# Issuing the sine half of the rotated q and k transfers from ScalarE's queue

## The chip, the cores and the metric

The kernel runs on one core of a Trainium2 chip. A core has five engines that run side by side, each with its own queue of instructions worked in order: TensorE (PE, matmuls; its weight loads are listed as PEld), VectorE (DVE), ScalarE (ACT), GpSimd (POOL) and SyncE (SP, which here only issues transfers). An engine waits at the head of its queue until what the instruction needs is there. Transfers are done by 16 DMA engines; some engine has to issue each. The metric is the device time of one execution in microseconds (us), lower is better.

## What is computed

The reference has two parts. The first is a gated linear attention with complex decay, per batch (4) and head (8), over 768 positions with 48 channels:

```python
mag = np.sqrt(a_re * a_re + a_im * a_im)
scale = np.minimum(mag, 0.999) / (mag + 1e-06)
a_re_n, a_im_n = (a_re * scale, a_im * scale)
for t in range(S):
    new_re = ar * S_re - ai * S_im
    new_im = ar * S_im + ai * S_re
    kv = np.einsum('bhd,bhe->bhde', k[:, :, t], v[:, :, t])
    S_re, S_im = (new_re + kv, new_im)
    y[:, :, t] = np.einsum('bhd,bhde->bhe', q[:, :, t], S_re)
```

(`ar`, `ai` are the scaled decay of position t.) The second takes the 3072 rows of 384 that come out of it through a feed-forward layer with weights of 384 x 2048 and 2048 x 384:

```python
h = x @ w_in
g = h * (1.0 / (1.0 + np.exp(-1.702 * h)))
return (g @ w_out).astype(np.float32)
```

## The kernel before

**Units.** The 4 x 768 positions are cut into 12 units of 256, numbered u = 0 to 11; three units make a batch entry. A unit goes through three stages. `prepare` turns the decay into factors: running products and running angles of each channel, the cosine and sine of the angles, and q and k scaled by the products and multiplied with cosine and with sine. `attend` computes scores, masks them and forms the outputs and the running state in two halves of 128 positions. `moe` does the feed-forward layer in eight slices i of 256 hidden columns, each in two halves f. This text writes Hu.i.f for the hidden product of a half (L794, nine matmuls; three of float32 in unit 0), g for its activation on ACT (L807, L803 in unit 0), and Ou.i.f for the output product (L827, six matmuls). There are two PSUM buffers for H, taken in turn by the slices, so H of slice i waits until g of slice i - 2 has been read.

**The transfers in question.** `prepare` works with channels on partitions, `attend` with heads beside each other. In between, transfers inside SBUF bring the products to rows per head, in `remap` (L658 to L667): five DMAs from one source tile, which holds 256 columns of q, 256 of k and one of decay (1539 elements a row for three row groups). There are two source tiles: x = 0 is `qr`, the products with the cosine, and goes to rows 0 to 47 of `qkh`; x = 1 is `qk`, the products with the sine, and goes to rows 64 to 111. Both hold q and k columns, so the two halves differ in cosine and sine. Unit 0 is prepared in two parts of 128 positions, so there are 13 cosine and 13 sine blocks of five DMAs. The scores (p_ps, L702) and the turned keys (k_ps, L748, copied by ACT to `kt`, L759) read `qkh`.

**Weights.** The float64 words of the weights come in 16 tiles (A0 to A7 of w_in, U0 to U7 of w_out), in the order A0, A1, U0, A2, U1, A3, U2, A4, U3, A5, U4, A6, U5, A7, U6, U7, through four buffers `raw`. Each is loaded (L472), one step on ACT (L474) and three on DVE (L475, L478, L481) make float32 of it, and only then can its buffer be loaded again. Later steps split the tiles in a high and a low half (L494, L499). All this happens while unit 0 is under way.

**The order.** All steps are first collected by `add` with an engine, a guessed duration, a rank and the tiles they read and write. `Plan.order` then runs a list scheduler over them many times and keeps the order that its own cost function likes best; the instructions are written out in this order, so each engine's queue is fixed at build time. The scheduler treats SP by itself (L176 to L180): a step there is a DMA, or `work` of them, and frees SP at once but for the issues.

Of the kernel before, what the change touches and what calls it, by code (L numbers as in the profile page):

```python
# [21 lines left out]
P = 128  # L22
L = 128
HL = 64
T = 256
H = 8
D = 48
NR = 3
# [5 lines left out]
E0 = 32  # L34
# [42 lines left out]

def lag(a, b):
    return LAG if b != "PE" else 0.0 if a == b else LAG_PE


class Plan:
# [31 lines left out]
    def forward(self, rank, stay):  # L114
# [16 lines left out]
        while done < len(ops):  # L131
# [41 lines left out]
                continue  # L173
            can[e].remove(pick)
            heapq.heapify(can[e])
            if e == "SP":  # L176
                free[e] = s + 0.06 + 0.65 * (ops[n][8] - 1)
                hw = max(hw, s + 0.06) + 0.47 * ops[n][8]
                dma = max(dma, hw + 0.6) + dur
                end = dma + 0.9  # L180
            else:
                if ops[n][5] not in (None, table):
                    dur += max(0.0, LOAD - (s - idle))
                    table = ops[n][5]
                if e == "PE":
                    dur += CHANGE if kinds[n] != kind else 0.0
                    kind = kinds[n]
                free[e] = end = clock.end(s, dur, ops[n][8]) if e == "PE" else s + dur
            if e == "ACT":
                idle = end  # L190
                if ops[n][7] is not None:
                    todo[ops[n][7]] -= 1
                    held = ops[n][7] if todo[ops[n][7]] else None
# [9 lines left out]
    def backward(self, when):  # L203
# [14 lines left out]
        while done < len(ops):  # L218
# [35 lines left out]
            else:  # L254
                n = heapq.heappop(can[e])[1]
            dur = ops[n][1]
            if e == "SP":
                free[e] = s + max(dur, 0.47)
                end = s + 0.9 + dur + 1.13
            else:  # L260
                if ops[n][5] not in (None, table):
                    dur += LOAD if table else 0.0
                    table = ops[n][5]
                free[e] = end = s + dur
# [9 lines left out]
    def time(self, order, load):  # L274

        ops = self.ops
        free = dict(FREE)
        ends = [0.0] * len(ops)
        table, hw, dma, idle = None, 0.0, 0.0, 0.7
        clock = Clock()  # L280
        kinds, kind = self.kinds, None
        for n in order:
            e, dur = ops[n][0], ops[n][1]
            s = max([free[e]] + [ends[d] + lag(ops[d][0], e) for d in ops[n][4]])
            if e == "SP":
                free[e] = s + 0.06 + 0.65 * (ops[n][8] - 1)
                hw = max(hw, s + 0.06) + 0.47 * ops[n][8]
                dma = max(dma, hw + 0.6) + dur
                ends[n] = dma + 0.9
                continue  # L290
            if ops[n][5] not in (None, table):
                dur += max(0.0, load - (s - idle))
                table = ops[n][5]
            if e == "PE":
                dur += CHANGE if kinds[n] != kind else 0.0
                kind = kinds[n]
            free[e] = ends[n] = clock.end(s, dur, ops[n][8]) if e == "PE" else s + dur
            if e == "ACT":
                idle = s + dur
        return max(ends)  # L300
# [37 lines left out]
def attention_moe(ctx: ExitStack, tc: tile.TileContext, qk_in, v, a_in, w_in, w_out, qn, kn, vn, an, bn, out):  # L338
# [185 lines left out]
    def prepare_part(u, i, a, b, np_, mag, den, rec, sp, qm, th, *keys):  # L524
# [4 lines left out]
        def ks(*xs):  # L529
            return [f"{x}.{s}" for x in xs for s in sub]  # L530
# [3 lines left out]
        def rk(stage):  # L534
            return prep_rank(u, i, stage)
# [107 lines left out]
        for x, (dst, kd, fac, kf) in enumerate(((rv, "qr", cs, k_cs), (qv, "qk", t, k_th))):  # L643
            for j in range(2):
                both(f"rot{x}{j}", u, i, rk(f"rot{x}"), qj[1 - x][j], qj[0][j], fac, ALU.mult,
                     r=ks(f"qk{j}") + kf, w=ks(f"{kd}{j}"))
            if u == i == 0 and x == 1:
                for k in range(WARM):
                    add("PE", 0.43, -WARM + k, lambda k=k, dst=dst: mm(
                        h_ps[0][:, k % 2, :], lhsT=ident, rhs=dst[:, k % NR, 0:T], start=True, stop=True  # L650
                    ), r=["qk0.0", "qk1.0"], w=["h0.0", "h0.1"])
            if b == T:
                add("POOL", 0.13, rk(f"rot{x}"), lambda dst=dst: pool.tensor_copy(out=dst[:, :, 2 * n], in_=f_a[:, u, :]),
                    r=[f"fa{u}.{i}"], w=[f"{kd}1.1"])
            add("SP", REMAP * nn / (2 * T), rk(f"rot{x}"), lambda dst=dst, x=x: remap(u, x, o, nn, dst),
                r=ks(f"{kd}0", f"{kd}1"), w=[f"H{hb_(u)}.{s}.{x}" for s in sub], name=f"remap{u}.{i}.{x}", work=5)

    def remap(u, x, o, nn, src):  # L658


        dst = qkh[hb_(u)][64 * x : 64 * x + D, H * o : H * (o + nn)].rearrange("d (h x) -> d h x", h=H)
        rest = D - E0
        for j in range(2):
            dma(out=dst[:, j * NR : (j + 1) * NR, :], in_=src[j * D : (j + 1) * D, :, :])  # L664
        dma(out=dst[0:E0, 2 * NR : H, :], in_=src[2 * D : P, 0:NR:2, :])
        for j in range(2):
            dma(out=dst[E0:D, 2 * NR + j, :], in_=src[2 * D + j * rest : 2 * D + (j + 1) * rest, 1, :])  # L667

    def attend(u):
        sps = spans(u)  # L670
# [497 lines left out]
```

## Time and profile before

| what | us |
|---|---|
| median of 3 runs | 593.93 |
| lowest and highest | 593.01, 596.69 |
| the profiled execution | 601.2 |
| its span, first to last instruction | 599.4 |
| PE busy in the span | 556.5 |
| DVE busy | 484.9 |
| ACT busy | 279.6 |
| mean granted clock of PE | 0.994 |

A profile is one execution, with the profiler on. Rows of the timeline begin with the start in us from the span's begin and the length in us, then engine, line, operation, output tile <- input tiles and a count; what stands in brackets is how long the engine had been idle and which work ended the wait. `SPq` is SP's queue, issuing a DMA; the transfer itself goes on after that. Lines are those of the kernel before. The DMA engines move 78.46 MB in the span, 77.52 MB of it from one queue, SP's.

### The profile page before, as it was taken

The page shows a single profiled execution, that of the slowest core. Times are in us where ns is not written, and L with a number is a line of the kernel's source. Part 1 is how long each engine was busy: PE and PEld are TensorE (multiplying, and loading weights), DVE is VectorE, ACT ScalarE, POOL GpSimd, SP SyncE. Part 2 cuts the span into 40 slices and gives each one's busy share as a digit, 9 for nine tenths or more (in the row PEclk, how much of TensorE's full clock was granted, in tenths as well). Part 3 has the DMA queues.
Part 4 walks back from the last instruction along what each step waited for, and adds up shares of the span by engine and source line. Part 5 has one row for each costly group of instructions (what it writes and reads, how often), then busy time and mean ns, then how long its engine had stood idle before and what let it go on. Part 6 is the DMA issues. An engine that isn't in the chain of part 4 may idle for free.

```text
span 599.4 us, 14244 instructions
## 1 busy us (share of the span) xinstructions
PE 556.5 (93%) x5804; PEld 513.8 (86%) x5804; DVE 484.9 (81%) x1003; ACT 279.6 (47%) x468; POOL 26.3 (4%) x75
## 2 busy tenths in 40 slices
PE   0489959999999999999999999999999999999997
PEld 0367637999998999989999989988999989999997
DVE  7999859998968988979979789869979889555543
ACT  7877457546337354354373552552473542211210
POOL 4110001000101000000010000000001000000000
PEclk9999979999999999999999999999999999999999
DMA  8479972272283362374670861772670732732110
GB/s 336 140 253 345 213 180 78 57 153 68 71 187 97 86 160 96 92 157 135 126 208 19 177 198 37 150 223 57 138 201 19 153 129 68 137 86 70 63 45 30
DMA packets 31525, 78.46 MB, mean 131 GB/s; under 512 B 4448, under 2 KB 9568, under 8 KB 31456
## 3 DMA queue, kind: packets, MB, share of 16 engines
q1 hardware_dynamic: 31456, 77.52, 48.3%
q8 instruction: 46, 0.75, 0.5%
q14 instruction: 23, 0.19, 0.1%
HBM read 53.87 MB, written 4.72 MB: 98 GB/s over the span
## 4 chain that ended last, share of the span: by engine, by line
PE 76%; DMA 10%; DVE 8%; ACT 2%; SPq 2%; issue 1%; DVEq 0%; ACTq 0%
PE h_ps L794 30%; PE o_ps L827 30%; PE x_ps L728 6%; PE p_ps L702 5%; DMA raw_w<-in_w_out_dram 4%; DMA raw_w<-in_w_in_dram 3%; PE k_ps L748 2%; PE z_ps L755 2%; DMA raw<-in_w_in_dram 2%; SPq L667 1%; DVE fit L854 1%; DVE s L616 1%; DMA raw<-in_w_out_dram 1%; SPq L664 1%; DVE qk L456 1%
## 5 line engine op out<-in xcount | busy, mean ns | idle before, releaser
L807 ACT ACTIVATE g<-h_ps 128x256 f32<-128x256 f32 x176 | 62.6, 382 | 219.6 <-PE h_ps L794 132.5
L794 PE MATMUL h_ps<-xhi,hiA 128*128 128x256 f32 x528 | 151.6, 287 | 1.6 <-issue 1.1
L794 PE MATMUL h_ps<-xlo,hiA 128*128 128x256 f32 x528 | 149.0, 282 | 0.0
L794 PE MATMUL h_ps<-xhi,loA 128*128 128x256 f32 x528 | 149.0, 282 | 0.0
L794 PEld LDWEIGHTS h_ps<-xhi,hiA 128*128 128x128 f32 x528 | 100.2, 190 | 4.0 <-issue 2.1
L794 PEld LDWEIGHTS h_ps<-xhi,loA 128*128 128x128 f32 x528 | 100.5, 190 | 0.0
L794 PEld LDWEIGHTS h_ps<-xlo,hiA 128*128 128x128 f32 x528 | 100.4, 190 | 0.2
L827 PE MATMUL o_ps<-hiU,gh 128*128 128x384 f32 x352 | 93.9, 346 | 1.4 <-DVE osb L838 1.0
L827 PE MATMUL o_ps<-loU,gh 128*128 128x384 f32 x352 | 89.6, 335 | 0.0
L827 PE MATMUL o_ps<-hiU,gl 128*128 128x384 f32 x352 | 89.6, 335 | 0.0
L810 DVE CAST gh<-g 128x256 fp32r<-128x256 f32 x176 | 48.9, 288 | 39.9 <-ACT g L807 35.6
L812 DVE TENSOR_TENSOR gl<-g,gh 128x256 fp32r<-128x256 f32 x176 | 72.1, 422 | 5.6
L827 PEld LDWEIGHTS o_ps<-loU,gh 128*128 128x128 f32 x352 | 63.7, 188 | 0.0
L827 PEld LDWEIGHTS o_ps<-hiU,gl 128*128 128x128 f32 x352 | 63.6, 188 | 0.0
L827 PEld LDWEIGHTS o_ps<-hiU,gh 128*128 128x128 f32 x352 | 58.2, 189 | 5.6 <-issue 2.0
L854 DVE TENSOR_REDUCE fit<-raw_w 128x1 f32<-128x256 f32 x96 | 38.2, 413 | 25.5 <-DMA raw_w<-in_w_out_dram 16.3
L456 DVE TENSOR_TENSOR qk<-qk,s 128x768 f32<-128x768 f32 (+1 forms) x52 | 46.0, 892 | 0.2
L1005 ACT ACT_TABLE_LOAD x35 | 44.9, 1283 | 1.4 <-PEq L1156 0.8
L702 PEld LDWEIGHTS p_ps<-qkh 128*64 128x64 f32 x768 | 36.4, 136 | 10.4 <-issue 4.5
L702 PE MATMUL p_ps<-qkh 128*64 128x128 f32 (+1 forms) x768 | 42.7, 252 | 2.2 <-DVE pm L706 2.2
L706 DVE TENSOR_TENSOR pm<-p_ps,mask 128x512 f32<-128x512 f32 x48 | 33.0, 688 | 10.8 <-PE p_ps L702 10.5
L728 PE MATMUL x_ps<-pm,v 128*32 128x128 f32 x768 | 38.2, 278 | 1.5 <-DVE pm L706 1.4
(94 smaller groups left out, 753.3 us busy)
## 6 DMA issues: line engine op xcount, KB each, us to landing
v<-in_v_dram SPq DMA_DIRECT2D x24, 352.0 KB, 4.0
ri<-in_a_dram SPq DMA_DIRECT2D x11, 768.0 KB, 5.0
qk<-in_qk_dram SPq DMA_DIRECT2D x11, 768.0 KB, 5.1
qkh<-qr SPq DMA_DIRECT2D x22, 288.6 KB, 5.8
qkh<-qk SPq DMA_DIRECT2D x22, 288.6 KB, 7.3
raw<-in_w_in_dram SPq DMA_DIRECT2D x8, 768.0 KB, 7.5
raw<-in_w_out_dram SPq DMA_DIRECT2D x8, 768.0 KB, 8.4
raw_w<-in_w_in_dram SPq DMA_DIRECT2D x24, 256.0 KB, 2.8
```

Of the source, the lines that this page charges most:

```text
L456: add(en, t, rank, lambda: e.tensor_tensor(out=out, in0=a, in1=b, op=alu), **kw)
L702: mm(p_ps[to : to + HL, j, lo:L], lhsT=at(h, 1, c)[:, lo : lo + HL], rhs=at(h, 0, c)[:, lo:L], start=True, stop=True)
L706: add("DVE", d_t(CW), rk(4 * c + hh), lambda hh=hh: dve.tensor_tensor(out=pm[hh].rearrange("p (a b) t -> p a b t", b=2), in0=p_ps.rearrang ...
L728: mm(x_ps[32 * j : 32 * j + 32, r, :], lhsT=lt, rhs=rt, start=n == 0, stop=n == len(steps) - 1)
L748: nc.tensor.transpose(k_ps[:, j, 0:KD], at(4 * hh + j, 1, c)[0:KD], ident[0:KD, 0:KD])
L794: mm(h_ps[hb][:, f, :], lhsT=ww[:, r * T + f * P : r * T + (f + 1) * P], rhs=x[:, r, :], start=n == 0, stop=n == last)
L807: add("ACT", a_t(T) - 0.15, rk(i), lambda hb=hb, f=f: act(out=g32[:, f, :], in_=h_ps[hb][:, f, :], func=AF.Silu, scale=SLOPE), r=[f"h{hb}. ...
L810: add("DVE", d_t(T, 2), rk(i), lambda gb=gb, f=f: dve.tensor_copy(out=high.g(gb)[:, f, :], in_=g32[:, f, :]), r=[f"g.{f}"], w=[f"gh{gb}.{f}"])
L812: add("DVE", d_t(T), rk(i), lambda gb=gb, f=f: dve.tensor_tensor(out=glo[gb][:, f, :], in0=g32[:, f, :], in1=high.g(gb)[:, f, :].bitcast(F ...
L827: mm(o_ps[t], lhsT=x[:, f, t * L : (t + 1) * L], rhs=y[:, f * DM : (f + 1) * DM], start=i == 0 and f == 0 and n == 0, stop=i == NP - 1 and ...
L854: add("DVE", d_t(CK), rk + 2, lambda x=x, op=op: dve.tensor_reduce(out=f_w[:, x, n : n + 1], in_=weights.looked_at()[:, :, 1], op=op, axis ...
L1005: nc.scalar.preload_act_table_set(o[5])
```

## The change

The sine blocks (x = 1) are issued from ACT's queue, the cosine blocks stay with SP. `remap` picks the queue by x, and the step is added to ACT with a kind "dma". The planner's three passes take such a step on ACT as an issue: it holds ACT for 0.65 us a DMA in the planner's count, and ends when the transfer has landed.

```diff
+def issue(e, n):
+    return 0.06 + 0.65 * (n - 1) if e == "SP" else (0.65 if e == "ACT" else 1.0) * n
...
-            if e == "SP":
-                free[e] = s + 0.06 + 0.65 * (ops[n][8] - 1)
+            if e == "SP" or kinds[n] == "dma":
+                free[e] = s + issue(e, ops[n][8])
                 hw = max(hw, s + 0.06) + 0.47 * ops[n][8]
                 dma = max(dma, hw + 0.6) + dur
                 end = dma + 0.9
+                if e == "ACT":
+                    idle = free[e]
...
-            add("SP", REMAP * nn / (2 * T), rk(f"rot{x}"), lambda dst=dst, x=x: remap(u, x, o, nn, dst),
-                r=ks(f"{kd}0", f"{kd}1"), w=[f"H{hb_(u)}.{s}.{x}" for s in sub], name=f"remap{u}.{i}.{x}", work=5)
+            add("ACT" if x else "SP", REMAP * nn / (2 * T), rk(f"rot{x}"), lambda dst=dst, x=x: remap(u, x, o, nn, dst),
+                r=ks(f"{kd}0", f"{kd}1"), w=[f"H{hb_(u)}.{s}.{x}" for s in sub], name=f"remap{u}.{i}.{x}", work=5, kind="dma")
...
+        queue = (nc.sync, nc.scalar)[x].dma_start
         for j in range(2):
-            dma(out=dst[:, j * NR : (j + 1) * NR, :], in_=src[j * D : (j + 1) * D, :, :])
-        dma(out=dst[0:E0, 2 * NR : H, :], in_=src[2 * D : P, 0:NR:2, :])
+            queue(out=dst[:, j * NR : (j + 1) * NR, :], in_=src[j * D : (j + 1) * D, :, :])
+        queue(out=dst[0:E0, 2 * NR : H, :], in_=src[2 * D : P, 0:NR:2, :])
```

Since the planner counts otherwise, the order changes on every engine, not only at the moved steps. Lines of the new kernel are 8 to 9 higher here (L664 becomes L673, L472 becomes L480). Three places matter below.

On SP at the start, before: the cosine and sine blocks of both parts of unit 0 stand in one row, and the next weight loads behind them.

```order
L664 DMA qkh_75<-qr 48x768 x2
L665 DMA qkh_75<-qr 32x2x256
L667 DMA qkh_75<-qr 16x256 x2
L664 DMA qkh_75<-qk 48x768 x2
L665 DMA qkh_75<-qk 32x2x256
L667 DMA qkh_75<-qk 16x256 x2
L664 DMA qkh_75<-qr 48x771 x2
L665 DMA qkh_75<-qr 32x2x257
L667 DMA qkh_75<-qr 16x257 x2
L664 DMA qkh_75<-qk 48x771 x2
L665 DMA qkh_75<-qk 32x2x257
L667 DMA qkh_75<-qk 16x257 x2
```

On ACT at the same place, now: both sine blocks stand behind the last sine of unit 0 (L650) and ahead of a square for unit 1, a weight step and the two `kt` copies.

```order
L650 ACTIVATE s_85<-s_85 128x3x128
L673 DMA qkh_75<-qk 48x768 x2
L674 DMA qkh_75<-qk 32x2x256
L676 DMA qkh_75<-qk 16x256 x2
L673 DMA qkh_75<-qk 48x771 x2
L674 DMA qkh_75<-qk 32x2x257
L676 DMA qkh_75<-qk 16x257 x2
L440 ACTIVATE s_81<-ri 128x3x256
L482 ACTIVATE raw_73<-raw_73 128x768
L768 ACTIVATE kt_97<-k_ps 128x448
L482 ACTIVATE raw_74<-raw_74 128x768
L768 ACTIVATE kt_97<-k_ps 128x448
```

Ten issues have gone from SP's row into ACT's, ahead of steps that PE's attention of unit 0 waits for.

On SP around unit 1's blocks, before: the load of A7 (into `raw_72`) stands between the cosine and the sine block, those of U6 and U7 behind both.

```order
L472 DMA raw_71<-in_w_out_dram 128x1536
L664 DMA qkh_75<-qr 48x1539 x2
L665 DMA qkh_75<-qr 32x2x513
L667 DMA qkh_75<-qr 16x513 x2
L472 DMA raw_72<-in_w_in_dram 128x1536
L664 DMA qkh_75<-qk 48x1539 x2
L665 DMA qkh_75<-qk 32x2x513
L667 DMA qkh_75<-qk 16x513 x2
L472 DMA raw_73<-in_w_out_dram 128x1536
L472 DMA raw_74<-in_w_out_dram 128x1536
```

The same place on SP now:

```order
L480 DMA raw_71<-in_w_out_dram 128x1536
L480 DMA raw_72<-in_w_in_dram 128x1536
L673 DMA qkh_75<-qr 48x1539 x2
L674 DMA qkh_75<-qr 32x2x513
L676 DMA qkh_75<-qr 16x513 x2
L480 DMA raw_73<-in_w_out_dram 128x1536
L480 DMA raw_74<-in_w_out_dram 128x1536
```

A7's load has moved ahead of the cosine block; U6's and U7's now follow it directly, and the sine block is no longer in this row.

On ACT in the feed-forward layer of unit 1, now: the sine block of unit 2 stands between the two g of slice 4 (h_ps_106 is the buffer of even slices), where before the g followed each other.

```order
L816 ACTIVATE g_98<-h_ps_107 128x256 x2
L816 ACTIVATE g_98<-h_ps_106 128x256
L673 DMA qkh_76<-qk 48x1539 x2
L674 DMA qkh_76<-qk 32x2x513
L676 DMA qkh_76<-qk 16x513 x2
L816 ACTIVATE g_98<-h_ps_106 128x256
L816 ACTIVATE g_98<-h_ps_107 128x256 x2
```

The other nine later blocks stand likewise between two g.

More of the change, by code (lines that the diff above doesn't have):

```diff
@@ L189, in forward @@
             if e == "ACT":
-                idle = end
+                idle = free[e]
                 if ops[n][7] is not None:
@@ L256, in backward @@
             dur = ops[n][1]
-            if e == "SP":
-                free[e] = s + max(dur, 0.47)
+            if e == "SP" or self.kinds[n] == "dma":
+                free[e] = s + max(dur if e == "SP" else 0.0, issue(e, ops[n][8]), 0.47)
                 end = s + 0.9 + dur + 1.13
@@ L284, in time @@
             s = max([free[e]] + [ends[d] + lag(ops[d][0], e) for d in ops[n][4]])
-            if e == "SP":
-                free[e] = s + 0.06 + 0.65 * (ops[n][8] - 1)
+            if e == "SP" or kinds[n] == "dma":
+                free[e] = s + issue(e, ops[n][8])
                 hw = max(hw, s + 0.06) + 0.47 * ops[n][8]
@@ L289, in time @@
                 ends[n] = dma + 0.9
+                if e == "ACT":
+                    idle = free[e]
                 continue
@@ L662, in remap @@
         rest = D - E0
+        queue = (nc.sync, nc.scalar)[x].dma_start
         for j in range(2):
-            dma(out=dst[:, j * NR : (j + 1) * NR, :], in_=src[j * D : (j + 1) * D, :, :])
-        dma(out=dst[0:E0, 2 * NR : H, :], in_=src[2 * D : P, 0:NR:2, :])
+            queue(out=dst[:, j * NR : (j + 1) * NR, :], in_=src[j * D : (j + 1) * D, :, :])
+        queue(out=dst[0:E0, 2 * NR : H, :], in_=src[2 * D : P, 0:NR:2, :])
         for j in range(2):
-            dma(out=dst[E0:D, 2 * NR + j, :], in_=src[2 * D + j * rest : 2 * D + (j + 1) * rest, 1, :])
+            queue(out=dst[E0:D, 2 * NR + j, :], in_=src[2 * D + j * rest : 2 * D + (j + 1) * rest, 1, :])
     def attend(u):
```

## The prediction

> **What bounds the kernel now.** I read the slices of the page first, then who waited for whom on TensorE (PE), then the chain of waits and the timeline where PE waits. In the slices (40 of 15 us) PE is full from the seventh on:
>
> ```profile
> PE   0489959999999999999999999999999999999997
> DVE  7999859998968988979979789869979889555543
> ACT  7877457546337354354373552552473542211210
> DMA  8479972272283362374670861772670732732110
> ```
>
> ```profile
> PE h_ps L649 <- DVE qk L456: 23.3, 1, 23.3
> PE h_ps L794 <- ACT g L803: 7.1, 1, 7.1
> PE p_ps L702 <- DVE pm L706: 2.2, 2, 1.3
> ```
>
> The waits of PE (us in total, times, longest) are two: 23.3 us before its first instruction and 7.1 us once. All that the change can win lies before some 100 us. The windows say the same (length, then busy us of PE, PEld, DVE, ACT, POOL; PE clock; DMA share; GB/s):
>
> ```profile
> 74.80:79.80 5.00, 0.00 (x0) 0.00 (x0) 0.00 (x0) 0.00 (x0) 0.00 (x0) 0.81 1.03 149
> 82.00:110.00 28.00, 28.00 (x333) 21.11 (x334) 25.69 (x41) 20.79 (x30) 2.22 (x5) 0.95 0.26 89
> 110.00:500.00 390.00, 384.71 (x4176) 364.14 (x4176) 335.23 (x699) 184.11 (x304) 12.86 (x45) 1.00 0.49 123
> ```
>
> From 74.8 to 79.8 no engine works and the DMA engines are full at 149 GB/s. The timeline shows why:
>
> ```profile
> 62.17 1.18 SPq L664 DMA_DIRECT2D qkh<-qr  x2
> 66.71 0.52 SPq L472 DMA_DIRECT2D raw<-in_w_in_dram  x1
> 67.94 3.10 SPq L664 DMA_DIRECT2D qkh<-qk  x2
> 70.75 1.45 PE L827 MATMUL o_ps<-valU,g 128*128 128x384 f32 x4
> 72.04 1.46 PE L794 MATMUL h_ps<-x,valA 128*128 128x256 f32 x6
> 73.23 1.51 SPq L667 DMA_DIRECT2D qkh<-qk  x2
> 79.81 0.56 DVE L475 TENSOR_SCALAR valA<-raw 128x768 int32<-128x768 int32 x1 [6.32 <-DMA raw<-in_w_in_dram]
> 79.87 0.92 ACT L474 ACTIVATE raw<-raw 128x768 int32<-128x768 uint32 x1 [7.59 <-DMA raw<-in_w_in_dram]
> 81.84 2.93 PE L794 MATMUL h_ps<-x,valA 128*128 128x256 f32 x6 [7.05 <-ACT g L803]
> 84.69 0.89 PE L702 MATMUL p_ps<-qkh 128*64 128x128 f32 x16
> ```
>
> ```profile
> 66.71 13.08 DMA raw<-in_w_in_dram
> ```
>
> The load of weight tile A7 is issued at 66.71 behind unit 1's cosine transfers and takes 13.08 us among them and the sine transfers; ACT stands in L474 for it, so the g that frees PE's buffer is late. PE waits 7.05 us, and the six matmuls behind the wait take 2.93 instead of 1.46: together 8.5 us.
>
> **The change, part by part.** It removes and adds no computation: 65 DMA issues go from SP to ACT, and the planner writes another order on every engine.
>
> Start of the work on PE:
>
> ```profile
> 21.71 1.23 SPq L664 DMA_DIRECT2D qkh<-qr  x2
> 23.31 7.51 PE L649 MATMUL h_ps<-qk,ident 128*128 128x256 f32 x26 [23.31 <-DVE qk L456]
> 25.05 1.17 SPq L664 DMA_DIRECT2D qkh<-qk  x2
> 30.66 0.55 PE L748 MATMUL k_ps<-ident,qkh 112*128 112x112 f32 x4
> 31.24 0.55 ACT L759 ACTIVATE kt<-k_ps 128x448 f32<-128x448 f32 x1
> 43.06 0.47 ACT L736 ACTIVATE x<-x_ps 128x384 f32<-128x384 f32 x1
> 49.53 1.21 ACT L803 ACTIVATE g<-h_ps 128x256 f32<-128x256 f32 x4
> 49.97 2.85 PE L827 MATMUL o_ps<-valU,g 128*128 128x384 f32 x8 [0.43 <-ACT g L803]
> ```
>
> A half's five issues take SP 25.05 - 21.71 = 3.3 us. The sine half waits for SP until 25.05; on ACT it goes out at about 23.2, when DVE has rotated it, and is 1.9 us earlier. That wins nothing: the 26 warm-up matmuls wait for the same rotation and hold PE until 30.7. I take 0, between 0 and +0.5. ACT pays for it: ten issues, 6.6 us, stand in front of a square, a weight step and the kt copy of 31.24.
>
> What ACT and DVE take for the steps that change places (a DVE step of the chain of waits each, one ACT step of the timeline, the table loads of the page):
>
> ```profile
> 53.27 0.47 DVE valA L475
> 53.74 0.87 DVE valU L481
> ```
>
> ```profile
> 80.69 0.83 ACT L494 ACTIVATE hiA<-valA 128x768 fp32r<-128x768 f32 x1
> ```
>
> ```profile
> L1005 ACT ACT_TABLE_LOAD x35 | 44.9, 1283 | 1.4 <-PEq L1156 0.8
> ```
>
> In the new order ACT has, between unit 0's second x copy and its first g, five steps like L494 (0.83), three L474 (0.92), the kt copy (0.55) and two table loads (1.28): 10.0 us, where the old one took 49.53 - 43.53 = 6.0. The copy itself comes earlier: of DVE's steps one like L475 and about 5.5 like L481, 5.4 us in all, move behind the last mask product ahead of it. I count half, 2.7. The term is 10.0 - 6.0 - 2.7 = **+1.3**, between -1.4 (all 5.4) and +5.4 (ten issues that end 4.1 later, see the second rival).
>
> The stall. A7's load now stands ahead of unit 1's cosine transfers, and the sine transfers have their own queue. Then its 13.08 us go to some 7, and the 7.05 of waiting and the 1.47 of slow matmuls go: **-8.5**, between -8.5 and 0. What is late next? ACT issues the five sine transfers between g of slices 4 and 5 of unit 0, 3.9 us (below). PE has about as much of its own there, an output half and two hidden halves, but the g ahead comes late too, behind ACT's step for A7: **+1.0**, between 0 and +3.8 (the five issues from 67.94 on took 6.8, to 74.74, 2.9 more). PE would then ask for unit 1's rotated rows at about 81.4: 74.79, plus 1.46 for the second half of slice 6, plus 2.85 for the output product that the new order puts first, plus 1.3 and 1.0.
>
> But those rows leave later than before. ACT comes to the issue behind g of slice 4, which PE's output half of 70.75 takes, now 70.75 + 1.3 + 1.0 = 73.0, and behind A7's L474 of 0.92: at 73.9 (before: 67.94). It ends at 77.8. How long the last piece flies:
>
> ```profile
> qkh<-qk SPq DMA_DIRECT2D x2, 32.1 KB, 9.4
> qkh<-qk SPq DMA_DIRECT2D x2, 32.1 KB, 5.5
> ```
>
> The first row is the DMA view of 60 to 80 us, the second that of 105 to 150 (copies, KB, median us to landing). So they land between 83.3 and 87.2, and PE, with half a us of z before it, waits 1.4 to 5.3. I take **+3.4**, the middle, since two weight loads stand beside them and not three. Last, U6's load now stands behind the cosine transfers where A7's stood; DVE may wait for it up to 6.3 us as it did for A7, most of it beside PE's own wait: **+1.0**, between 0 and +6.3.
>
> Units 1 to 10. Each has one such block on ACT. How long it is, and what PE has to do meanwhile:
>
> ```profile
> 160.53 1.16 SPq L664 DMA_DIRECT2D qkh<-qr  x2
> 164.44 1.16 SPq L664 DMA_DIRECT2D qkh<-qk  x2
> 203.68 1.16 SPq L664 DMA_DIRECT2D qkh<-qr  x2
> ```
>
> ```profile
> 113.33 2.17 PE h_ps L794 x18
> 115.50 4.16 PE o_ps L827 x24
> ```
>
> Rows 1 and 2 (timeline) give 3.9 us for five issues, the last two (chain of waits) 1.08 us for one hidden half and 1.04 for one output half. At the tightest place, unit 1, PE has after H1.4.1 (unit, slice, half) three hidden and four output halves, 7.4 us, before it needs that half's buffer again; ACT, blocked 3.9 us from 0.7 us before H1.4.1's end, has g ready at 3.6. So **0**. Nothing in the order stands between the sine rotation on DVE and this place, so ACT should not wait for data. The new order's own gaps I bound by what PE lacks in the window of 110 to 500 us, 390 - 384.71 = 5.3 us, either way.
>
> Sum: 1.3 - 8.5 + 1.0 + 3.4 + 1.0 + 0 = -1.8. The span goes from 599.4 to 597.6 and the profiled execution from 601.2 to 599.4; the median of the runs shown, 593.93, is 7.3 below that execution and becomes **592.1**.
>
> **Rivals.** *The stall goes whole.* If the sine rows, on a queue of their own, have landed when PE comes, the last two terms fall: -6.2, and -8.5 without the two delays on ACT: 587.7 to 585.4. For it: the landings of 5.5 us where the DMA engines have room. Against: the DMA row of the slices has 9 from 45 to 75 us.
>
> *Two queues share one issuer.* Then SP's and ACT's issues take turns. The twenty at the start end at 21.7 + 20 x 0.62 = 34.1 and not at 23.2 + 10 x 0.66 + 0.2 of waiting = 30.0, all behind them on ACT comes 4.1 later, the first term is +5.4 and the sum +2.3: 596.2. For it: rows of SP issue back to back at 0.6 us each, and nothing in this trace issues from two queues at once. Against: no row shows whether that 0.6 belongs to SP or to something shared. The Trainium skill, "Perfetto Trace Analysis", section "DMA Instruction — HWDGE (DVE, Sync)", says that such an instruction first waits for a lock on a generator of descriptors that the queues share; by that rule this rival holds. "DMA: Bandwidth & Descriptors", section "Issuing engines are not separate DMA queues", adds that transfers of all issuers run on the same 16 engines and that only issuing time is saved, which speaks against the first rival. No run so far shows either.
>
> *DVE becomes the bound.* While ACT issues, DVE stands at its next cast of g. A unit takes 43.2 us (160.53 to 203.68); DVE works 335.23 of 390, or 37.1 of 43.2, so ACT's block fits up to 6.1 us a unit. At 6.8 (67.94 to 74.74) each of ten units would lose 0.7, at twice 3.9 1.7: +7 to +17 on the sum of -1.8, so 599 to 609, middle 604. For it: DVE's order puts other steps behind a cast that waits. Against: outside the full stretch SP shows 3.9.
>
> **How the numbers follow.** Forecast 0.44 (own range 589 to 595), the stall goes whole 0.21, shared issuer 0.22, DVE bound 0.13. A measurement of this kernel tells about 1%, 5.9 us, from no change. Faster by more: the first rival, 0.21. Slower by more: the last, 0.13. The rest, 0.66. The range reaches from the first rival's end over the shared issuer's 596.2 with its gaps of 3.7: 585.4 to 600.
>
> **What would show it.** In the changed profile: PE's first k_ps near 30.7; first g of unit 0 at 50 to 51; no wait of 7 us before L803; instead a wait of PE at unit 1's p_ps for rows still in flight, its p_ps between 83 and 88; five issues on ACT of about 3.9 us in later units and no new wait of PE there. I am wrong if PE is full before 80, if an issue on ACT takes much over 0.8 us, or if PE's gaps after 110 us grow past 10 us in all.

## The result and the profile after

| | median us | lowest to highest | runs |
|---|---|---|---|
| before | 594.26 | 593.01 to 596.69 | 4 |
| changed | 629.09 | 625.38 to 629.92 | 4 |

The changed kernel is slower, by a ratio of 1.055 (95% interval 1.051 to 1.059): 34.8 us where 1.8 us of gain were forecast. Its profiled execution took 629.92 us, with a span of 628.1 us, PE busy for 567.6 of them and a mean granted clock of 0.978.

The slices of the changed kernel (40 of 15.7 us), for TensorE (PE), VectorE (DVE), ScalarE (ACT) and PE's granted clock:

```profile
PE   0587979999999999999899899679999979999997
...
DVE  6969979997958889688699689366869959665543
ACT  7378848546355383543453632441335344221110
...
PEclk9988979999999999999999999789999989999999
```

PE is no longer full from the seventh slice on. It has holes in the later units, and around slice 26 its clock falls too. The windows of 110 to 500 us (length, then busy us of PE, PEld, DVE, ACT and POOL; PE clock; DMA share; GB/s) put a number on it:

```profile
110.00:500.00 390.00, 372.00 (x3930) 350.55 (x3929) 317.80 (x660) 171.65 (x288) 8.98 (x40) 0.99 0.44 113
```

PE lacks 18.0 us there, where it lacked 5.3 before. The waits of PE in the changed kernel (us in total, times, longest):

```profile
PE h_ps L657 <- DVE qk L464: 23.5, 1, 23.5
PE h_ps L803 <- ACT g L816: 11.4, 6, 4.9
PE o_ps L836 <- ACT g L812: 8.4, 2, 4.2
PE x_ps L737 <- DVE pm L715: 3.5, 2, 3.2
PE z_ps L764 <- ACT kt L768: 3.3, 1, 3.3
PE k_ps L757 <- ACT kt L768: 2.9, 3, 1.9
```

Apart from the unchanged first row, nearly all of it is waiting for ACT: g and kt. ACT's own waits say where it was:

```profile
ACT g L816 <- DMA qkh<-qk: 43.0, 6, 10.7
ACT g L812 <- DMA qkh<-qk: 10.1, 1, 10.1
ACT s L440 <- DMA qkh<-qk: 9.9, 1, 9.9
ACT kt L768 <- DMA qkh<-qk: 7.9, 1, 7.9
```

These four rows are nine of the twelve blocks of sine transfers (unit 0's two stand together): time in which ACT does nothing else between two steps. The rows of ACT and its queue (ACTq) in two of them, the first in unit 1, the second in unit 8:

```profile
76.76 0.37 ACT L812 ACTIVATE g<-h_ps 128x256 f32<-128x256 f32 x1
77.24 1.19 ACTq L673 DMA_DIRECT2D qkh<-qk  x2
78.47 1.07 ACTq L674 DMA_DIRECT2D qkh<-qk  x1
85.89 1.20 ACTq L676 DMA_DIRECT2D qkh<-qk  x2
87.20 0.66 ACT L812 ACTIVATE g<-h_ps 128x256 f32<-128x256 f32 x2 [10.07 <-DMA qkh<-qk]
...
389.83 1.29 ACTq L673 DMA_DIRECT2D qkh<-qk  x2
391.17 1.30 ACTq L674 DMA_DIRECT2D qkh<-qk  x1
395.96 1.20 ACTq L676 DMA_DIRECT2D qkh<-qk  x2
397.27 0.38 ACT L816 ACTIVATE g<-h_ps 128x256 f32<-128x256 f32 x1 [10.71 <-DMA qkh<-qk]
```

The issues themselves take about 0.6 us each, as forecast, the single one, L674, 1.07 and 1.30. But between the third and the fourth there is a hole: 78.47 + 1.07 = 79.5 to 85.89 in unit 1, 392.5 to 395.96 in unit 8. What the fourth waits for is written in the compiled program. The transfers of SP and ACT, counted together in program order, signal their landing on eight semaphores in turn, DMAHW0 to DMAHW7, and a transfer is not issued before the one eight places earlier, which used the same semaphore, has landed. The block of unit 8 in ACT's queue (row number, line, transfer, what it waits for):

```
363 L673 DMA qkh_76<-qk 48x1539 [waits DMAHW0_49,DMAHW6_49,DVE_49,Pool_49]
364 L673 DMA qkh_76<-qk 48x1539 [waits DMAHW2_49]
365 L674 DMA qkh_76<-qk 32x2x513 [waits DMAHW5_49]
366 L676 DMA qkh_76<-qk 16x513 [waits DMAHW0_49]
367 L676 DMA qkh_76<-qk 16x513 [waits DMAHW1_49]
```

Row 366 is transfer 184 of the program, and the landing it waits for on DMAHW0 is that of transfer 176: row 363, ACT's own first sine transfer of the same block. The DMA view of the changed kernel for 389.8 to 390.2 us (copies, KB, us to landing) has that one:

```profile
qkh<-qk ACTq DMA_DIRECT2D x1, 288.6 KB, 6.1
```

Issued at 389.83, it lands 6.1 us later, at 395.9; the fourth issue starts at 395.96. In unit 1 the same pair is 77.24 and a landing of 8.6 us, so 85.8; the fourth starts at 85.89. So ACT does not only issue, it stands until one of its own transfers has flown. From the first issue to ACT's next step the eleven blocks of units 1 to 11 take 75.3 us in all, 3.9 to 10.0 and 6.8 in the mean, where the forecast had 3.9. The rows of their issues are 41.0 us of it, as much as SP's rows for the same transfers took in the kernel before (41.0); the holes between the issues are 33.0.

On SP such waits were there before and cost nothing by themselves, since nothing urgent stood behind them. The prediction's row of 3.10 us for two issues at 67.94 holds one: the second issue starts at 70.53. The next issue starts at 72.24, and the cosine transfer eight places ahead of it, issued at 62.17, landed at 72.2. But the waits were shorter: 6.4 us in SP's eleven sine blocks before, 4.1 of them in unit 1, and 2.4 in the first kernel below, which has the changed order with every transfer on SP. There unit 8's sine block stands behind the whole cosine block:

```profile
378.49 1.16 SPq L673 DMA_DIRECT2D qkh<-qr  x2
385.00 1.45 SPq L676 DMA_DIRECT2D qkh<-qk  x2
```

The transfer eight places ahead of the one issued at 385.00 is the first cosine transfer, issued 6.5 us earlier, and it has landed by then. With two queues SP and ACT take the eight semaphores in turn, so the eighth ahead of row 366 had left only 2.6 us before ACT was ready for it. Issuing side by side is what makes the wait long.

### The profile page after: what moved, and what is told of

Same layout as the page of the kernel before. It is cut to its first block, busy times and chain, and to the rows that moved or that the text cites. A ratio compares the mean times of both kernels' runs of the same rounds, so it can differ in the third digit from the quotient of the medians.

```text
span 628.1 us, 14280 instructions
## 1 busy us (share of the span) xinstructions
PE 567.6 (90%) x5804; PEld 521.1 (83%) x5804; DVE 487.1 (78%) x1003; ACT 278.5 (44%) x468; POOL 21.9 (3%) x75
## 2 busy tenths in 40 slices
DMA packets 31526, 78.47 MB, mean 125 GB/s; under 512 B 4448, under 2 KB 9568, under 8 KB 31456
## 5 line engine op out<-in xcount | busy, mean ns | idle before, releaser
L816 ACT ACTIVATE g<-h_ps 128x256 f32<-128x256 f32 x176 | 62.2, 382 | 235.4 <-PE h_ps L803 126.4
L803 PE MATMUL h_ps<-xhi,hiA 128*128 128x256 f32 x528 | 154.0, 292 | 11.5 <-ACT g L816 11.4
L803 PEld LDWEIGHTS h_ps<-xhi,hiA 128*128 128x128 f32 x528 | 101.7, 193 | 15.4 <-ACT g L816 13.3
L803 PEld LDWEIGHTS h_ps<-xlo,hiA 128*128 128x128 f32 x528 | 102.0, 193 | 0.3
L803 PEld LDWEIGHTS h_ps<-xhi,loA 128*128 128x128 f32 x528 | 102.1, 193 | 0.0
L711 PE MATMUL p_ps<-qkh 128*64 128x128 f32 (+1 forms) x768 | 44.1, 258 | 2.7 <-DVE pm L715 2.7
```

Source lines behind the costliest of these rows:

```text
L711: mm(p_ps[to : to + HL, j, lo:L], lhsT=at(h, 1, c)[:, lo : lo + HL], rhs=at(h, 0, c)[:, lo:L], start=True, stop=True)
L803: mm(h_ps[hb][:, f, :], lhsT=ww[:, r * T + f * P : r * T + (f + 1) * P], rhs=x[:, r, :], start=n == 0, stop=n == last)
L816: add("ACT", a_t(T) - 0.15, rk(i), lambda hb=hb, f=f: act(out=g32[:, f, :], in_=h_ps[hb][:, f, :], func=AF.Silu, scale=SLOPE), r=[f"h{hb}. ...
```

## The experiments

Four theories. Theory 1: ACT stands at its issues because each waits for the landing of an earlier transfer, and that costs once ACT's absence in a unit is longer than the work around it can bridge. Theory 2: the planner's new order is the worse one, whatever queue issues. Theory 3: the plain time of the issues on ACT is enough. Theory 4: two queues share the DMA engines, and rows land late. Line numbers shift by a few from kernel to kernel.

**The order and the queue, each alone.** The first kernel keeps the changed order and issues everything from SP:

```diff
-        queue = (nc.sync, nc.scalar)[x].dma_start
+        queue = nc.sync.dma_start
```

> The changed kernel's order on every engine, but all ten transfers of a unit issued from SP again. Theory 1 (ACT stands at its own issues, because a transfer on its queue has to wait until the eighth transfer before it has landed): no block on ACT, time 587 to 600 us, the wait of 7.05 us for A7 gone, PE's waits for g under 8 us in all. Theory 2 (the new order itself is the worse one): 620 to 632 us, as the changed kernel. Theory 3 (ACT stands there, but the plain 3.9 us of five issues are enough for the loss): as theory 1.

Measured: 605.68 us, ratio to before 1.015 (1.008 to 1.022). The second is the kernel before, planner and order included, with the line `queue = (nc.sync, nc.scalar)[x].dma_start` in `remap`, used by its five transfers:

> The kernel before with its own order, only the five sine transfers of each block issued from ACT. Theories 1 and 3: slower, 615 to 640 us (A7's stall stays and the blocks on ACT come on top); by theory 1 the block of a unit is 6 to 8 us long from its first issue to ACT's next step, with the gap behind the second or third issue; by theory 3 it is 3.9 to 4.5 us. Theory 2: 594 to 600 us.

Measured: 641.91 us, ratio 1.076 (1.067 to 1.084), just above the 615 to 640 of theories 1 and 3, and blocks on ACT of 3.9 to 9.7 us. So the queue is the larger part in either order. Between the first kernel and the changed one, which differ in nothing but the queue, lie 629.09 - 605.68 = 23.4 us. The order alone costs 605.68 - 595.96 (before in the same session) = 9.7 us, more than theories 1 and 3 allowed: theory 2 holds for a smaller part.

**Issue time or wait.** The next kernel is the changed one, but in all eleven units after the first (the expectation says ten) the cosine transfers are left out. That shifts which transfer is the eighth before each of ACT's; ACT's five issues stay:

```diff
+        if u and not x:
+            return
         queue = (nc.sync, nc.scalar)[x].dma_start
```

> The changed kernel without the five cosine transfers of units 1 to 10 (their rows in qkh keep older values). The eighth transfer before each of ACT's is then a load or a store that left long before. Theory 1: ACT's block is 3.9 to 4.5 us long without a gap, time 592 to 604 us. Theory 3: the five issues stay, so 620 to 632 us. Theory 4 (the rows land late because two queues share the DMA engines): also faster, but with the gaps between ACT's issues kept in part.

Measured: 606.29 us, ratio 1.014 (1.007 to 1.022), a little above the 592 to 604 of theory 1, which had left out what the order costs. The block of unit 8 in ACT's timeline:

```profile
379.94 1.17 ACTq L675 DMA_DIRECT2D qkh<-qk  x2
381.15 1.27 ACTq L676 DMA_DIRECT2D qkh<-qk  x1
382.46 2.12 ACTq L678 DMA_DIRECT2D qkh<-qk  x2
384.68 0.38 ACT L818 ACTIVATE g<-h_ps 128x256 f32<-128x256 f32 x1 [8.00 <-DMA qkh<-qk]
```

The hole of 3.5 us is gone. The eleven blocks take 45.6 us, 4.1 in the mean, with 42.6 in the rows and 1.8 in holes, and the time is that of the order alone. Five plain issues on ACT thus cost about nothing, as the prediction had it, and theory 3 falls. It also has less traffic, so by itself it doesn't exclude theory 4.

The next kernel is the changed one with all its traffic, but the last three of the five sine transfers, those with the long waits, go back to SP:

```diff
-        queue(out=dst[0:E0, 2 * NR : H, :], in_=src[2 * D : P, 0:NR:2, :])
+        dma(out=dst[0:E0, 2 * NR : H, :], in_=src[2 * D : P, 0:NR:2, :])
...
-            queue(out=dst[E0:D, 2 * NR + j, :], in_=src[2 * D + j * rest : 2 * D + (j + 1) * rest, 1, :])
+            dma(out=dst[E0:D, 2 * NR + j, :], in_=src[2 * D + j * rest : 2 * D + (j + 1) * rest, 1, :])
```

> The changed kernel's order, with only the first two of the five sine transfers issued from ACT and the last three from SP. Theory 1 (the waits of the third to fifth for an earlier transfer are what costs): ACT's block 1.2 to 1.5 us, time 602 to 609 us, as with all on SP. Theory 3 (the plain issue time costs): two fifths of the loss stay, 612 to 618 us.

Measured: 602.71 us, ratio 1.010 (1.006 to 1.014); from first issue to ACT's next step 1.4 to 3.7 us. The loss beside the order is gone, with two queues at work.

**How long may ACT be away.** Three kernels have the changed order, every transfer on SP, and on ACT in the place of the five issues, in units 1 to 11, dependent copies of the mask onto itself, which change no value (10, then 14 and 18 in the place of 10):

```diff
-        queue = (nc.sync, nc.scalar)[x].dma_start
+        queue = nc.sync.dma_start
+        for _ in range(10 if u and x else 0):
+            act(out=mask, in_=mask, func=AF.Copy)
```

> All transfers from SP (as in the run with the order alone, 605.7 us), and on ACT, where the five issues stood in units 1 to 10, ten dependent copies of the mask onto itself, about 4 us by the rows of g (0.38 us each). Theory 1 with a slack (a block of ACT costs nothing up to some 5 to 6 us a unit, then each us counts): 603 to 611 us. If every us of a block costs in proportion (23.4 us for 75 us): 616 to 621 us.

> The same with fourteen copies, about 5.6 us a block, just at the slack. With a slack: 606 to 618 us. In proportion: 621 to 627 us.

> The same with eighteen copies, about 7.2 us a block, beyond the slack and near the mean of 6.8 us of the changed kernel, without any transfer on ACT. With a slack: 618 to 636 us, with PE waiting for g and its clock low behind those waits, as in the changed kernel. If the loss came from the transfers (two queues, late landings) and not from ACT's absence: 605 to 612 us.

| copies | ACT away in a unit, us | time, us | over the order alone | DVE's waits for g, us |
|---|---|---|---|---|
| 0 | 0 | 605.68 | | 32.0 |
| 10 | 4.4 | 608.62 | +2.9 | 38.6 |
| 14 | 6.2 | 613.59 | +7.9 | 50.5 |
| 18 | 8.0 | 635.36 | +29.7 | 68.6 |

The last column is a row of DVE's waits; in order, for 0, 10, 14 and 18 copies and, last, for the changed kernel:

```profile
DVE gh L819 <- ACT g L816: 32.0, 24, 3.0
```
```profile
DVE gh L821 <- ACT g L818: 38.6, 32, 3.0
```
```profile
DVE gh L821 <- ACT g L818: 50.5, 33, 3.6
```
```profile
DVE gh L821 <- ACT g L818: 68.6, 35, 5.4
```
```profile
DVE gh L819 <- ACT g L816: 58.4, 34, 4.9
```

The loss is no straight line: little up to about 4 us a unit, and from 6.2 to 8.0 us another 22 us, 2 us of time in each unit for 1.8 us of absence. In the mean of the units that is a slack which is used up near 6 us. PE's waits for g (L816 there, L818 here) with 18 copies are those of the changed kernel and more, without a transfer on ACT:

```profile
PE h_ps L805 <- ACT g L818: 16.1, 7, 5.9
```

The blocks of the changed kernel differ in length, so one more kernel gives ACT as many copies in each unit as fill that unit's block there:

```diff
-        for _ in range(10 if u and x else 0):
+        for _ in range((0, 22, 9, 15, 11, 17, 12, 17, 17, 15, 17, 17)[u] if x else 0):
```

> The order alone on SP (605.7 us) with copies of the mask on ACT in each unit after the first, as many as fill that unit's block in the changed kernel at 0.44 us each (22, 9, 15, 11, 17, 12, 17, 17, 15, 17, 17 for blocks of 10.0, 3.9, 6.8, 5.0, 7.5, 5.2, 7.6, 7.4, 6.7, 7.6, 7.6 us). If ACT's absence is the whole loss beside the order: 622 to 635 us. If a part of the 23.4 us comes from rows that land late because two queues share the DMA engines: 608 to 620 us.

Measured: 622.9 us, ratio 1.050 (1.041 to 1.059), with copies for 74.6 us in all against 75.3. ACT's absence alone is 622.9 - 605.7 = 17.2 of the 23.4 us (the two were measured apart; as ratios to the kernel before they are 1.050 and 1.015). Two more kernels ask whether the remaining 6 us lie in unit 0, where the replay has no copies. The first issues the sine transfers of unit 0 alone from ACT, the second those of the later units alone, both in the changed order:

```diff
-        queue = (nc.sync, nc.scalar)[x].dma_start
+        queue = (nc.sync, nc.scalar)[x and not u].dma_start
```

> The changed kernel's order, with the ten sine transfers of unit 0 issued from ACT and those of all later units from SP. If the 6 us that the replayed blocks left open lie in unit 0's two blocks (9.3 us on ACT): 607 to 611 us (605.7 plus about 3, the lag of PE's first products of units 0 and 1 against the replay). If unit 0's blocks cost nothing: 604 to 607 us.

```diff
-        queue = (nc.sync, nc.scalar)[x].dma_start
+        queue = (nc.sync, nc.scalar)[x if u else 0].dma_start
```

> The changed kernel's order, with the ten sine transfers of unit 0 issued from SP and those of all later units from ACT. ACT's absence alone gave 622.9 us with the same blocks. If unit 0 is the rest: 622 to 627 us. If the rest lies in later units, beside ACT's absence: 627 to 631 us.

Measured: 606.02 us (ratio 1.017, 1.009 to 1.024) and 627.51 us (1.056, 1.048 to 1.064). Unit 0's two blocks, 9.5 us on ACT in this run, cost nothing at the end, and nearly all the loss is in the later units. About 5 us of it, 627.5 - 622.9, is not ACT's absence as the copies make it, but the intervals of the two ratios overlap. Late landings may be a part of that; it stays open.

Where the loss arises can be read from PE's turned keys. This is their first row for unit 10, with the order alone and in the changed kernel:

```profile
492.29 0.60 PE L757 MATMUL k_ps<-ident,qkh 112*128 112x112 f32 x4
```
```profile
516.29 0.60 PE L757 MATMUL k_ps<-ident,qkh 112*128 112x112 f32 x4
```

The same for other units, as us behind the order alone (what a block costs may show only at the next unit):

| unit | 1 | 2 | 5 | 6 | 7 | 9 | 10 | 11 |
|---|---|---|---|---|---|---|---|---|
| block on ACT, changed kernel | 10.0 | 3.9 | 7.5 | 5.2 | 7.6 | 6.7 | 7.6 | 7.6 |
| behind, changed kernel | 6.7 | 6.7 | 6.1 | 9.8 | 9.7 | 18.2 | 24.0 | 24.3 |
| behind, copies of the same length | 2.4 | 3.5 | 4.3 | 9.7 | 11.2 | 11.6 | 16.5 | 16.9 |
| behind, 18 copies in every unit | 1.4 | 5.2 | 9.2 | 17.2 | 19.2 | 21.3 | 27.8 | 28.6 |

The loss comes in steps, and length alone does not set them: 8.0 us of copies in every unit cost 8.0 us from unit 5 to 6 and 0.8 from unit 10 to 11. So the 6 us are a mean, and each unit has a slack of its own. Of the 7.3 us by which the changed kernel's profile ends behind that of the replay, 4.3 stand already at unit 1; why is not shown.

**POOL as the issuer.** The cosine transfers of the changed kernel from POOL, whose transfers have eight semaphores of their own:

```diff
-        queue = (nc.sync, nc.scalar)[x].dma_start
+        queue = (nc.gpsimd, nc.scalar)[x].dma_start
```

> The changed kernel with all transfers kept, the cosine ones issued from POOL, whose transfers count on semaphores of their own, so the eighth before each of ACT's is mostly a load that left earlier. Theory 1: ACT's block 3.9 to 5 us, time 595 to 610 us, if POOL's issues (no row shows their price) do not make the cosine rows late. Theory 3: 620 to 632 us. Theory 4: 615 to 632 us, since the traffic is unchanged.

Measured: 629.17 us, ratio 1.053 (1.044 to 1.062), where theory 1 said 595 to 610. The blocks are short, 51.1 us for eleven, but ACT stands 21.5 us in front of them. In unit 1 that wait comes from this, in POOL's timeline:

```profile
74.71 1.03 POOL L673 DMA_DIRECT2D qkh<-qr  x2 [14.53 <-DVE valA L483]
75.75 0.57 POOL L674 DMA_DIRECT2D qkh<-qr  x1
76.32 0.98 POOL L676 DMA_DIRECT2D qkh<-qr  x2
77.29 6.90 POOL L661 COPY qk<-fit 128x3 f32<-128x3 f32 x1
```

The copy that completes the sine source stands on POOL behind the cosine issues and ends at 84.19; ACT's first issue starts at 84.22. So the next kernel moves this copy, for the sine rows, to DVE:

```diff
-                add("POOL", 0.13, rk(f"rot{x}"), lambda dst=dst: pool.tensor_copy(out=dst[:, :, 2 * n], in_=f_a[:, u, :]),
+                add("POOL", 0.13, rk(f"rot{x}"), lambda dst=dst, x=x: (pool, dve)[x].tensor_copy(out=dst[:, :, 2 * n], in_=f_a[:, u, :]),
```

> The run with the cosine transfers on POOL, with the small copy of the decay into the sine rows moved from POOL (where it stood behind the five issues and took up to 6.9 us, so that ACT waited 21.5 us in all ahead of its own issues) to DVE. All traffic is kept and both queues issue. Theory 1: ACT's blocks 3.9 to 5.5 us with 5 to 8 us of waiting ahead of them in all, time 603 to 613 us. Theory 4 (two queues make the rows land late): 620 to 632 us.

Measured: 627.08 us, ratio 1.050 (1.041 to 1.058): a miss again. The wait in front of the blocks fell to 6.2 us in all, the blocks took 57.2 us, and yet the time stayed. The holes are gone as theory 1 has it (1.8 us in the eleven blocks), but the rows are longer, 54.1 us instead of 41.0. Read unit by unit between the rows of the table of copies, such blocks would cost some 6 to 7 us, an estimate, and not 21. Some 4 us are the end of the program, shown below for another kernel with transfers on POOL. What this run has beside that is rows in flight: the large sine transfers take 8.6 us to land (median of the page; 6.8 with everything on SP, 7.4 in the changed kernel), and PE waits for them:

```profile
PE p_ps L711 <- DMA qkh<-qk: 4.9, 4, 2.3
```

So with three queues theory 4 has some weight, and this pair did not isolate theory 1. The other way round, the kernel before in its own order with the sine transfers on POOL:

```diff
+        queue = (nc.sync, nc.gpsimd)[x].dma_start
...
-            dma(out=dst[:, j * NR : (j + 1) * NR, :], in_=src[j * D : (j + 1) * D, :, :])
+            queue(out=dst[:, j * NR : (j + 1) * NR, :], in_=src[j * D : (j + 1) * D, :, :])
```

The transfers of the two lines below are edited in the same way.

> The kernel before with its own order, the five sine transfers of each block issued from POOL, with semaphores of its own and almost nothing behind them. Theory 1 (what costs is who stands behind the issues): 588 to 600 us, no block on ACT; PE's wait for A7 between 4 and 8 us, since its load still leaves behind the cosine transfers. If POOL's issues hold up POOL's own later steps (a copy of 0.13 us took 6.9 us behind five of them in the run with the cosine transfers there) so that DVE or ACT wait for them: 600 to 615 us.

Measured: 604.41 us, ratio 1.011 (1.004 to 1.019), outside the range of theory 1. The stall that the forecast wanted to win is gone in this run, against the expectation, and the kernel is still not faster. Its PE timeline:

```profile
75.78 1.56 PE L795 MATMUL h_ps<-x,valA 128*128 128x256 f32 x6 [0.57 <-ACT g L804]
...
78.77 0.60 PE L749 MATMUL k_ps<-ident,qkh 112*128 112x112 f32 x4
79.21 1.47 PE L828 MATMUL o_ps<-valU,g 128*128 128x384 f32 x4
83.64 1.55 PE L703 MATMUL p_ps<-qkh 128*64 128x128 f32 x16 [2.96 <-DVE pm L707]
...
87.88 2.65 PE L828 MATMUL o_ps<-valU,g 128*128 128x384 f32 x4
...
97.61 0.60 PE L749 MATMUL k_ps<-ident,qkh 112*128 112x112 f32 x4
```

The same points in the kernel before:

```profile
85.52 0.60 PE L748 MATMUL k_ps<-ident,qkh 112*128 112x112 f32 x4
...
98.41 0.60 PE L748 MATMUL k_ps<-ident,qkh 112*128 112x112 f32 x4
```

PE waits 0.57 instead of 7.05 us for g, and unit 1's turned keys come 6.75 us earlier (78.77 against 85.52). But then PE waits for DVE's mask product, its matmuls run slow behind that wait (2.65 for four where 1.47 is usual), and 19 us later the lead is 98.41 - 97.61 = 0.8 us.

About half of this run's loss is not in the work at all. PE's last matmul ends at 597.2 us, 1.7 later than in the kernel before (595.5), but the span goes on for 8.0 us behind it, where the kernel before has 3.9. One of POOL's last instructions, a DRAIN, takes 5.5 us here (shortest, median, longest in ns), and at most 0.08 before:

```profile
L1165 POOLq DRAIN  x3: 34/107/5526, 598.9 to 605.0; - x3
```
```profile
L1164 POOLq DRAIN  x3: 34/45/82, 597.2 to 599.1; - x3
```

Both kernels with the cosine transfers on POOL show the same: 5.4 us of DRAIN, and 7.6 and 7.9 us behind the last matmul.

**The planner.** The changed kernel with the price of an issue on ACT set to the mean that was seen:

```diff
-    return 0.06 + 0.65 * (n - 1) if e == "SP" else (0.65 if e == "ACT" else 1.0) * n
+    return 0.06 + 0.65 * (n - 1) if e == "SP" else (1.36 if e == "ACT" else 1.0) * n
```

> The changed kernel with one number of the planner's rules changed: an issue on ACT counts as 1.36 us instead of 0.65, so a block of five as 6.8 us, the mean that the changed kernel showed. If the loss is a price that the planner could have planned around: 598 to 618 us. If it is not a fixed price but a wait for landings that no constant describes: 620 to 640 us, with blocks on ACT between 4 and 10 us as before.

Measured: 622.16 us, ratio 1.043 (1.035 to 1.051), with blocks of 4.2 to 9.1 us. That is 7 us better than the changed kernel, and at the lower end of what was expected of a wait that no constant describes.

All transfers on SP, and only the units after the first planned as if on ACT:

```diff
-        queue = (nc.sync, nc.scalar)[x].dma_start
+        queue = nc.sync.dma_start
...
-            add("ACT" if x else "SP", REMAP * nn / (2 * T), rk(f"rot{x}"), lambda dst=dst, x=x: remap(u, x, o, nn, dst),
+            add("ACT" if x and u else "SP", REMAP * nn / (2 * T), rk(f"rot{x}"), lambda dst=dst, x=x: remap(u, x, o, nn, dst),
```

> All transfers issued from SP, and the planner told that only those of the units after the first cost ACT time, so that unit 0 is ordered without them. If the 9.7 us that the order alone costs come from the start (first g of unit 0 at 54.6 us where it was 49.5): first g at 49 to 51 us, time 594 to 601 us. If they come from the order of the later units: 601 to 608 us.

Measured: 603.17 us, ratio 1.013 (1.005 to 1.020); the first g of unit 0 stands at 47.98 us, 6.6 earlier than with the order alone (54.61). The end moved by 2.5 us; their spreads (600.6 to 604.0 and 605.6 to 607.7) do not touch, but as ratios to the kernel before, 1.013 and 1.015, the two are not told apart. So most of what the order costs is not in the start.

The kernel before once more, for a second profile:

> The kernel before, unchanged, for a second profile: the profiled execution shown first took 601.2 us where the runs' median was 594. Expected 593 to 597 us, with PE's two waits (23.3 us at the start, 7 us for A7) as they were, so that the other order can be compared with an ordinary execution.

Measured: 602.21 us in the profiled execution, above the 593 to 597 expected, with a span of 600.5 and PE's two waits as they were (23.3 and 7.3). Both profiled executions of this kernel are thus 6 to 7 us longer than the median of its others, while those of the order alone and of the order of the later units are at their medians. Set against their spans of 603.8 and 600.6 us, the profiles show only 0 to 4 of the order's 8 to 10 us. Where the rest lies stays open.

No version that was tried is faster than the kernel before.

## Why the prediction was wrong

The step that failed is the length of a block on ACT: "Rows 1 and 2 (timeline) give 3.9 us for five issues", hence 0 for units 1 to 10 and +1.0 for unit 1's block. Rows of an issue were taken as its price. They show how long the issuing takes, not what the issue waits for first, and on SP such a wait looks like idle time of a queue with nothing to do. The trace had a sign of it: five issues that took SP 6.8 us at 67.94. The prediction used them as an upper bound and did not ask what stood between them. The Trainium skill, "Perfetto Trace Analysis", section "DMA Instruction — HWDGE (DVE, Sync)", puts the reported start of such an instruction behind its wait for semaphores; the trace agrees, with 6.4 us between the third and fourth issue in unit 1 that belong to no row. Against the order alone the two terms measure 23.4 us instead of 1.0; by the turned keys 6.7 us stand at unit 1 and the rest in the later units. Copies of the same length on ACT lose 17.2 of the 23.4; what the other 6 are stays open.

- **The slack and the third rival.** The forecast gave the block a room of 6.1 us a unit before DVE would become the bound. A room of about that size was there in the mean: copies of 6.2 us cost 7.9 us, of 8.0 us 29.7, and DVE's wait for g grows with them. That it is DVE which ends the room is not shown: PE's own waits are for ACT's g, and the room differs from unit to unit. What was wrong is the length of the block, 6.8 us in the mean and up to 10.0 instead of 3.9, and with it the chance of 0.13. The price of 599 to 609 us was also low: at 6.8 us it counted 0.7 us a unit, and the replay, with such blocks, lost 17.2 us in eleven units, 1.6 each. Why it was more is not shown. Unequal blocks may lose more than their mean, since those above the slack cost and those below give nothing back. PE's clock falls behind some waits and not behind others: in the changed kernel the granted clock was 0.52 from 398 to 404 us, behind the wait of 4.9 us that follows unit 8's block, but 1.00 from 305 to 312, where a wait of 2.9 us lies.
- **The stall, -8.5.** The wait of 7.05 us for A7 did go, as forecast: in the changed kernel ACT's step for A7 starts at 75.93. But the gain was mis-sized. With the stall removed and nothing else in the order changed (sine transfers on POOL), 6.75 us were won at unit 1 and 0.8 were left at 98 us; the 4 us at the end of that kernel have no part in this. "What is late next?" was answered with ACT and the flight of the rows; it was DVE, with the mask product.
- **Unit 1's block, +1.0, and the landing wait, +3.4.** Expected: ACT's issues from 73.9 to 77.8 and PE at the scores between 83 and 88. They went from 77.24 to 87.20, and the wait moved from the scores to g. In the order with everything on SP unit 1's turned keys come at 88.92 us; in the changed kernel at 95.64.
- **First g, +1.3.** It came at 55.37 instead of 49.53, so +5.8; with the order alone at 54.61. ACT's second copy of x was counted 2.7 us earlier, for DVE's steps that move behind it (0.47 + 5.5 x 0.87 is 5.3 and not 5.4, which changes little); with the order alone it came at 43.76, 0.7 later than before. Like the stall it didn't count in the end: 6.6 us of it undone moved the end by 2.5.
- **The new order's own gaps, up to 5.3 either way.** 9.7 us: too small a bound. It was made from PE's gaps in one profiled execution, and the median of that kernel's other executions is 6 to 7 us shorter. The range's upper end, 600, counted only 3.7 of gaps, for which no row is named; with the 5.3 of the text it would have been 601.5.
- **Two queues share one issuer.** Not seen where the rival needed it. From 23.41 to 25.86 us, with both queues issuing, the rows of SP and ACT show six issues in 2.45 us, 0.4 each, where taking turns at 0.62 would have allowed four. By the rule of "Perfetto Trace Analysis" in the Trainium skill, same section, an issue first waits for a lock on a generator that the queues share, and that wait lies inside the reported time, so rows that had to take turns would have grown. Three of these four are as long as SP's alone were (1.23 for two, 0.69 and 0.65 for one), one pair is 0.4 longer (1.62 against 1.22): at most a small part of what that rival needed. In later units some rows are long where both queues issue, most in unit 7 (1.48 and 2.29 us for one issue each on ACT), but the sum of ACT's rows, 41.0 us, is that of SP's before.

```profile
23.50 0.69 SPq L674 DMA_DIRECT2D qkh<-qr  x1
24.24 1.62 SPq L676 DMA_DIRECT2D qkh<-qr  x2
```
```profile
23.41 1.24 ACTq L673 DMA_DIRECT2D qkh<-qk  x2
24.69 0.67 ACTq L674 DMA_DIRECT2D qkh<-qk  x1
```

- **The start on PE, 0.** Right: the first turned keys at 31.5 us instead of 30.7, and issuing unit 0's sine transfers from ACT cost 606.0 against 605.7 us.

Of the signs named in advance two told of the failure: PE's gaps after 110 us grew past 10 us (18.0), and no wait came at unit 1's scores. The third, issues of much over 0.8 us, could not tell: the single issue L674 took 0.81 to 2.29 us on ACT in units 1 to 11, but the same issue (L665) took 0.65 to 1.46 on SP before, and the lost time is between the issues.

## What to carry to other kernels

Before an instruction is moved to another queue, read all that it waits for in the compiled program, a reused completion semaphore of an earlier transfer included: on a queue with nothing behind it such a wait is free, on a compute engine everything behind it stands as long as a transfer flies. Two queues that draw on the same semaphores in turn make such a wait longer (33.0 us of holes here, 2.4 with all on SP). Then ask how long that engine may be away in one round of the pipeline; dummy work in the same place gives that number directly, and here it showed a slack of some 6 us of 43 in the mean, different from unit to unit, behind which the loss climbs steeply. And where a stall is to be won, follow it to the next engine that is nearly as late: here 6.75 us won at one point were 0.8 us after another 19.

## What the runs showed of the hardware

- Who issues hardly matters for the flight of the large sine transfers: they took 7.3 us to land (median of the page) from SP in the kernel before, 7.4 from ACT and 7.3 from POOL. The smallest (32.1 KB) differ: 5.8, 4.1 and 7.5. The Trainium skill, "DMA: Bandwidth & Descriptors", section "Issuing engines are not separate DMA queues", says that only issuing time is saved; the medians of the large ones agree.
- An issue on POOL took 0.5 us (1.03 for two), no more than on SP, but a copy of 128 x 3 elements behind five of them took 6.9 us in unit 1 and 4.0 in unit 2, over 1 us in three more units, and 0.2 to 0.7 in the others; in the kernel before such copies took 0.2 to 0.9.
- Transfers issued from POOL put some 4 us on the end of the program: POOL's DRAIN took 5.4 to 5.5 us in the three kernels that have them, and at most 0.08 in the kernel before.
